# Computing grad_out x gate x w2 of two chunks early and merging two MLP stages, in a transformer block's forward and backward

## The chip, the cores and the metric

The kernel runs on one NeuronCore of a Trainium2 chip. The core has a matrix engine (TensorE, "PE", with its weight loads as "PEld"), a vector engine (VectorE, "DVE"), an activation engine (ScalarE, "ACT"), GpSimd ("POOL"), and SyncE ("SP"), which only issues transfers. Each engine works through its own instructions in order; they meet at semaphores. The metric is the time of one execution on the device, in microseconds (us); lower is better. The kernel before took 2512.56 us in the median of three runs (2511.92 to 2516.4).

## The reference: what is computed

One adaptive-layernorm transformer block, forward and backward, in bf16, with one sequence of S = 2048 tokens, width D = 512, 32 heads of 16, and an MLP of width F = 1792 with squared ReLU:

```
mod = silu(c) @ w_mod               # six rows: sa, ca, ga, sb, cb, gb
h  = layernorm(x) * (1 + ca) + sa
x1 = x + ga * attention(h, wqkv, wo)
h2 = layernorm(x1) * (1 + cb) + sb
r  = relu(h2 @ w1 + b1)
out = x1 + gb * ((r * r) @ w2 + b2)
grads = vjp(block)(grad_out)        # to x, all weights, b1, b2, c, w_mod
```

Of the backward pass this matters here: with s = r * r, the gradient to s is ds = (grad_out * gb) @ w2^T; the one to r's input is dz = 2 * r * ds; the weight gradients are dw2 = s^T @ (grad_out * gb) and dw1 = h2^T @ dz; then dh = dz @ w1^T goes on into the second layernorm. ds needs neither the attention nor the forward MLP: grad_out, the gate gb and w2 are inputs, or follow from inputs at the start. gb has one value for each of the 512 columns.

## The kernel before

Partition size is P = 128. The MLP width is FC = 14 blocks of 128, D is DC = 4 blocks, the tokens are QC = 4 chunks of 512.

**Forward loop** (41.7 to 1006 us). The attention is a list of NF = 512 units (chunk of queries, group of 4 heads, block of 128 keys). In unit u, `fscore` computes the scores of four heads (L560, four matmuls into two PSUM tiles psST, three buffers) and their exponentials on ACT (L562, two ET of 128x1024), and `fpv` multiplies those of unit u-2 with the values (L576). In the same unit other work is slipped in between, in an order that the Python loop fixes by hand (the pools run under a manual schedule, so program order is engine order):
- `plan_tasks` (u = 0 to about 101, only in chunk 0's attention): keys, queries, norms and modulation rows, by `at(u, task)`.
- `later_stage`, when u % 4 == 2: a list of stages. Stage 24 falls on u = 106 (four L705, L706, L707 on DVE: the normalized input of 512 tokens), stage 25 on u = 110 (two reciprocals of one row of 512, L697).
- `turn_weights`, when u % 4 == 0, i = u/4 - 18: transposing DMAs of w1 (i = 2 to 5), of w2 and wo (i = 7 to 10), issued by SP; at i = 12 all three are stored to DRAM.
- `step(u)` moves on the generator `dense_chunk` by one yield, or runs one waiting weight-gradient chain. While chunk c+1's attention runs, `dense_chunk(c)` does chunk c's MLP, forward and backward: 14 steps of pz = w1^T h2 (L398) with relu and square, w2T loaded into the place of w1 (`load_wA`), 14 steps of pds = w2T x gfT (L412; gfT is grad_out * gb, transposed) with dz = 2 * pds * r (L415, which also sums dz for the bias gradient), then dh, the forward product and the attention gradient. A yield of n makes `step` wait n units.
- `steady`, when none of these has issued a product in the unit: two matmuls with zeros that add nothing (L599).

All of this work's products share one PSUM bank (`mm`, one buffer) in the loop. A **chain** (`add_chain`) is one tile of a weight gradient: four accumulating matmuls (L233) of 512, 384 or 256 columns, and its result. Chunk 0 stores the tile to DRAM (`p_st`), chunks 1 and 2 accumulate onto it, and chunk 3 adds it from SBUF (L237 on DVE, after `fetch_part` has loaded it) and writes the output with a DMA issued on ACT's queue. Chains wait in the list `dwq`; `later(n, ...)` issues something n units, or ticks, on.

**Between the loops** (1006 to 1124 us) the last chunk has no attention to hide behind. Here `mm` has four buffers and chains have three banks of their own (pc). `late_finish` and the head of `last_chunk` finish the attention and do the second layernorm. Then stage one: 14 steps of pz (L1336), relu (L1338, ACT), square (L1339, DVE), `tick` (what is due, and one chain) and `turn` (four transposes of s, L1323, evicted on ACT, L1324, and the chain of that block appended). Stage two: 14 steps of pds (L1351), dz (L1354, DVE), bias sum (POOL), `tick`, `turn` of dz. Then dh (L1377), the layernorm gradient, the forward product (L1429) and the attention gradient. `head_loads` issues the first loads of the next loop.

**Backward loop** (1124 to 2380 us): attention's backward by heads, in which ACT (L1601) and DVE (L1617) are both busy; then a final stage. The diff does not touch them.

Of the kernel before, what the change touches and what calls it, by code (L numbers as in the profile page):

```python
# [15 lines left out]
ALU = mybir.AluOpType  # L16
# [18 lines left out]
def kernel(  # L35
# [111 lines left out]
    with ExitStack() as ph:  # L147
# [32 lines left out]
        def later(lag, f, *args):  # L180
            due.append((unit[0] + lag, f, args))
# [108 lines left out]
        def chunk_loads(c):  # L290
            ts = slice(4 * c, 4 * c + 4)
            end = c == QC - 1
            if end:
                L = dict(begun)
            else:
                L = {"w1": load_wA(w1_src, 6), "w1T": load_wB(w1T_st[:], 20)}
                L["g"] = cb.tile([P, 4, D], BF, name="g_c", tag="g_c")
                sp(L["g"][:], g_dram[:, ts, :])
            L["wo"] = ffw.tile([P, DC, D], BF, name="wo_nat", tag="wo")
            sp(L["wo"][:], A_wo.rearrange("(oc p) j -> p oc j", p=P))  # L300
            L["x1"] = cb.tile([P, 4, D], BF, name="x1_c", tag="x1_c")
            sp(L["x1"][:], x_dram[:, ts, :])
            L["gf"] = cb.tile([P, 4, D], BF, name="gf_c", tag="gf")
            L["gfT"] = cb.tile([P, 4, DC, P], BF, name="gfT", tag="gfT")

            def scaled():
                POOL.tensor_tensor(L["gf"][:], L["g"][:], gb_bc.unsqueeze(1).to_broadcast([P, 4, D]), ALU.mult)
                later(6, sp, L["gfT"].rearrange("p t o q -> p (t o) q"), flat(L["gf"]), True)

            def sums():  # L310
                for ti in range(4):
                    rowsum(4, L["g"][:, ti, :], 4 * c + ti)

            if end:
                return L
            later(5, scaled)
            later(16, sums)
            return L

        def dense_chunk(c, O_c, L):  # L320
            ts = slice(4 * c, 4 * c + 4)
            g_c, x1_c, gf_c, gfT, w1_nat, w1T = (L[key] for key in ("g", "x1", "gf", "gfT", "w1", "w1T"))
            a_c = cb.tile([P, 4, D], BF, name="a_c", tag="a_c")
# [71 lines left out]
            for fc in range(FC):  # L395
# [9 lines left out]
                yield 0  # L405
            w2T = load_wA(w2T_st[:], 1)
            yield 3
            dzT = rT
            for fc in range(FC):
                pds = mm()  # L410
                for oc in range(DC):
                    PE.matmul(pds[:], w2T[:, oc, fc * P:(fc + 1) * P], gfT[:, :, oc, :],  # L412
                              start=(oc == 0), stop=(oc == DC - 1))
                db1p = wk.tile([P, 1], F32, name="db1p", tag="db1p")
                DVE.scalar_tensor_tensor(out=dzT[:, fc, :], in0=pds[:], scalar=2.0, in1=rT[:, fc, :],  # L415
                                         op0=ALU.mult, op1=ALU.mult, accum_out=db1p[:])
# [298 lines left out]
        def turn_weights(i):  # L715
            if i == 2:
                turned["1"] = ffw.tile([P, FC, D], BF, name="w1T_0", tag="wB")
                turned["2"] = ffw.tile([P, DC, FF], BF, name="w2T_0", tag="wA")
                turned["o"] = ffw.tile([P, DC, D], BF, name="woT_0", tag="wo")
            if 2 <= i < 6:  # L720
                for fc in range(4 * (i - 2), min(FC, 4 * (i - 2) + 4)):
                    sp(turned["1"][:, fc, :], B_w1[:, fc * P:(fc + 1) * P], True)
            if 7 <= i < 11:
                sp(turned["2"][:, i - 7, :], B_w2[:, (i - 7) * P:(i - 6) * P], True)
                sp(turned["o"][:, i - 7, :], A_wo[:, (i - 7) * P:(i - 6) * P], True)
# [262 lines left out]
        def plan_tasks():  # L988
# [124 lines left out]
            at(67, lambda: mod_cols_of(mm(), 3, 2))  # L1113

        NF = len(funits)

# [34 lines left out]
        with ExitStack() as ph2:  # L1151
# [3 lines left out]
            with tc.manual_schedule(engines={PE.engine, ACT.engine, DVE.engine, SP.engine, POOL.engine}):  # L1155
                fh[0, 0] = (qts[0], kts[0])
                for u in range(NF + 2):
# [75 lines left out]

        def last_chunk(O_c, L, w1T, w2T):
            c = QC - 1
            ts = slice(4 * c, 4 * c + 4)
            g_c, x1_c, gf_c, gfT, w1_nat = (L[key] for key in ("g", "x1", "gf", "gfT", "w1"))
            OT, pas = L["OT"], L["pa"]
# [74 lines left out]
            sT = cb.tile([P, FC, 512], BF, name="sT", tag="sT")  # L1313
            tks = {}

# [17 lines left out]
            for fc in range(FC):  # L1333
                pz = mm()
                for ic in range(DC):
                    PE.matmul(pz[:], w1_nat[:, ic, fc * P:(fc + 1) * P], h2T[:, :, ic, :],  # L1336
                              start=(ic == 0), stop=(ic == DC - 1))
                ACT.activation(rT[:, fc, :], pz[:], AF.Relu, bias=b1col[:, fc:fc + 1])  # L1338
                DVE.tensor_tensor(sT[:, fc, :], rT[:, fc, :], rT[:, fc, :], ALU.mult)  # L1339
                tick()  # L1340
                if fc > 0:
                    turn("s", sT, fc - 1)
            later(3, sp, woT[:], woT_st[:])
            w2_nat = ffw.tile([P, FC, D], BF, name="w2_1", tag="wA")
            for s in range(7):
                later(5 + 2 * s, sp, w2_nat[:, 2 * s:2 * s + 2, :], w2_src[:, 2 * s:2 * s + 2, :])
            dzT = rT
            for fc in range(FC):
                pds = mm()
                for oc in range(DC):  # L1350
                    PE.matmul(pds[:], w2T[:, oc, fc * P:(fc + 1) * P], gfT[:, :, oc, :],  # L1351
                              start=(oc == 0), stop=(oc == DC - 1))
                db1p = wk.tile([P, 1], F32, name="db1p", tag="db1p")
                DVE.scalar_tensor_tensor(out=dzT[:, fc, :], in0=pds[:], scalar=2.0, in1=rT[:, fc, :],  # L1354
                                         op0=ALU.mult, op1=ALU.mult, accum_out=db1p[:])
                POOL.tensor_tensor(db1acc[:, fc:fc + 1], db1acc[:, fc:fc + 1], db1p[:], ALU.add)
                if fc == 7:
                    head_loads()
                tick()
                turn(*(("dz", dzT, fc - 1) if fc else ("s", sT, FC - 1)))  # L1360
            turn("dz", dzT, FC - 1)
            keep["KS"] = kpool.tile([P, TT, QPAD], BF, name="KS_tok", tag="ks")
            POOL.memset(keep["KS"][:, :, D:QPAD], 0.0)
            for i in range(4):
                later(4 + 3 * i, sp, keep["KS"][:, 4 * i:4 * i + 4, 0:D], k_st[:, 4 * i:4 * i + 4, :])
            ACT.activation(tiny[:], onesf[:, 0:1], AF.Exp)
# [127 lines left out]
        with ExitStack() as ph2:  # L1494
            pools["mm"] = ph2.enter_context(tc.tile_pool(name="psM2", bufs=4, space=bass.MemoryType.PSUM))
            with tc.manual_schedule(engines={PE.engine, ACT.engine, DVE.engine, SP.engine, POOL.engine}):
# [11 lines left out]
                O_c = late_finish()  # L1508
                sp(L["gfT"].rearrange("p t o q -> p (t o) q"), flat(L["gf"]), True)
                for i in range(4):  # L1510
# [20 lines left out]

                last_chunk(O_c, L, w1T, w2T)
                for j, row in ((0, 5), (1, 3), (2, 4), (3, 2)):
# [518 lines left out]
```

## Time and profile before

| | us |
|---|---|
| median of three runs | 2512.56 (2511.92 to 2516.4) |
| span of the profiled execution (the page gives no other time of it) | 2513.8 |
| PE busy / ACT busy / DVE busy in the span | 2335.0 / 2302.6 / 1809.7 |
| ET, L562, 1024 times | 942.3 |
| first pz of stage one, first pds of stage two | 1024.38, 1051.90 |
| first dh product, first score of the backward loop | 1077.66, 1124.05 |

How to read it. Times are us from the span's start. A line of groups gives line, engine, operation, tiles with shapes and count, then busy time, mean ns of one, and the idle time just before, with what ended most of it. A line of the timeline gives start and duration; the bracket is the idle time before it and the engine, tile and line that ended it. In a row of stretches each engine has its busy time and, as (x), its instructions; the clock column is the TensorE clock granted, 1.00 being full speed; the DMA share is the mean busy share of 16 queues' engines, with GB/s behind it. Matmuls overlap: four of 128x512 show 1.03 us of busy time, but the next product can start 0.865 us after the first.

### The profile page before, as it was taken

The numbers are of one execution on the slowest core, as the hardware profiler recorded it, in microseconds if no ns is written. First come the engines' busy times: TensorE is split into PE (matmuls) and PEld (weight loads), VectorE is DVE, ScalarE is ACT, GpSimd is POOL, SyncE is SP. The second block draws the span as 40 slices with busy tenths as digits, with TensorE's granted clock in tenths as the row PEclk, the third lists the DMA queues.
The fourth block names the chain that finished last, engine by engine and source line by source line (L and its number), as shares of the span: only waits on it lengthen the run. The fifth ranks groups of instructions, "written<-read, shape, count | busy, mean of one in ns | idle before, by whom it ended". The sixth has DMA issues, their size and how long they took to land.

```text
span 2513.8 us, 49777 instructions
## 1 busy us (share of the span) xinstructions
PE 2335.0 (93%) x18916; PEld 777.9 (31%) x19005; DVE 1809.7 (72%) x2317; ACT 2302.6 (92%) x3577; POOL 348.0 (14%) x370
## 2 busy tenths in 40 slices
PE   7898889989988998999999999999999999999999
PEld 3232223222322323442233322233222323222343
DVE  6555153455435454579999999999998999999872
ACT  7999999999999999539999999999999999999952
POOL 2000000210333142210111101011010110110100
PEclk9999999999999999999999999999999999999999
DMA  6476465356748765969999999999999999999972
GB/s 203 129 193 177 136 131 139 96 160 136 110 88 174 153 131 118 264 211 184 207 203 210 199 198 204 204 201 206 204 200 206 199 195 204 206 199 215 197 254 72
DMA packets 1220981, 447.15 MB, mean 178 GB/s; under 512 B 1096951, under 2 KB 1191607, under 8 KB 1220486
## 3 DMA queue, kind: packets, MB, share of 16 engines
q1 hardware_dynamic: 1192822, 409.11, 81.8%
q0 software_dynamic: 10944, 16.78, 4.5%
q10 hardware_dynamic: 16976, 18.07, 2.8%
q8 instruction: 149, 2.44, 0.4%
q14 instruction: 90, 0.74, 0.1%
HBM read 96.75 MB, written 73.95 MB: 68 GB/s over the span
## 4 chain that ended last, share of the span: by engine, by line
PE 40%; ACT 39%; issue 7%; DVE 7%; DMA 4%; SPq 2%; ACTq 1%; POOL 0%; DVEq 0%; another core or an unknown queue 0%
ACT E_u L1601 24%; ACT ET L562 11%; PE dqacc L1682 5%; PE psST L560 4%; PE psS_A L1595 3%; PE pm L233 3%; PE accVK L1655 2%; ACT dsT L1761 2%; PE oacc L576 2%; PE psS_B L1595 2%; SPq L178 2%; PE psS_C L1595 2%; PE pm L412 2%; PE pdh L1876 2%; PE pwq L1910 2%
## 5 line engine op out<-in xcount | busy, mean ns | idle before, releaser
L1617 DVE TENSOR_TENSOR dS_u<-psD_u,E_u 128x1024 bf16<-128x1024 f32 x1024 | 1186.2, 1219 | 71.2 <-PE psD_u L1615 25.5
L562 ACT ACTIVATE ET<-psST 128x1024 bf16<-128x1024 f32 x1024 | 942.3, 1247 | 25.3 <-PE psST L560 24.7
L1601 ACT ACTIVATE E_u<-psS_A 128x512 bf16<-128x512 f32 x768 | 509.6, 664 | 11.0 <-PE psS_C L1595 8.5
L1601 ACT ACTIVATE E_u<-psS_B 128x512 bf16<-128x512 f32 x768 | 502.6, 654 | 12.5 <-PE psD_u L1615 3.4
L1615 PE MATMUL psD_u<-iv,ido 32*128 32x512 bf16 x2048 | 409.9, 388 | 0.5 <-DVE dS_u L1617 0.2
L560 PE MATMUL psST<-qt_sb,kt_sb 32*128 32x512 bf16 x2048 | 316.5, 387 | 53.0 <-ACT ET L562 46.2
L1601 ACT ACTIVATE E_u<-psS_C 128x512 bf16<-128x512 f32 x512 | 333.7, 652 | 2.7 <-PE psS_B L1595 1.0
L1595 PE MATMUL psS_B<-ik,iq 32*128 32x512 bf16 x768 | 294.9, 384 | 12.5 <-ACT E_u L1601 5.0
L1595 PE MATMUL psS_A<-ik,iq 32*128 32x512 bf16 x768 | 293.4, 382 | 11.1 <-DVE dwlast L237 1.0
L1595 PEld LDWEIGHTS <-iq 32*128 32x128 bf16 x2048 | 130.5, 91 | 316.0 <-issue 299.9
L1655 PE MATMUL accVK<-dS_u,qz 128*32 128x512 bf16 x2048 | 213.0, 390 | 0.5 <-PE psD_u L1615 0.3
L576 PE MATMUL oacc<-ET,vaug 128*32 128x512 bf16 x2048 | 207.8, 396 | 1.9 <-DVE ostage L580 1.9
L1664 PE MATMUL accVK<-E_u,dOs_tok 128*16 128x512 bf16 x2048 | 203.7, 386 | 0.0
L1700 POOL TENSOR_TENSOR dQacc<-dQacc,dqtmp 128x512 f32<-128x512 f32 x64 | 81.3, 1271 | 851.4 <-ACT dqtmp L1695 851.4
L1595 PE MATMUL psS_C<-ik,iq 32*128 32x512 bf16 x512 | 194.6, 380 | 4.2
L560 PEld LDWEIGHTS <-kt_sb 32*128 32x128 bf16 x2048 | 85.4, 91 | 341.0 <-issue 320.4
L1682 PE MATMUL dqacc<-dsT,KS_tok 128*32 128x512 bf16 x2048 | 147.7, 387 | 18.7 <-DMA dsT<-dS_u 4.3
L1761 ACT ACTIVATE dsT<-ptT 128x1024 bf16<-128x1024 bf16 x128 | 145.3, 1135 | 7.0 <-PE ptT L1645 6.4
L251 DVE COPY part<-pm 128x512 f32<-128x512 f32 (+2 forms) x103 | 63.5, 617 | 117.5 <-PE pm L233 106.0
L1615 PEld LDWEIGHTS <-ido 32*128 32x128 bf16 x2048 | 105.0, 91 | 100.7 <-issue 94.5
L1655 PEld LDWEIGHTS <-qz 128*32 128x32 bf16 x2048 | 58.5, 94 | 177.8 <-issue 162.8
L576 PEld LDWEIGHTS <-vaug 128*32 128x32 bf16 x2048 | 53.0, 93 | 121.0 <-issue 121.0
(407 smaller groups left out, 2499.5 us busy)
## 6 DMA issues: line engine op xcount, KB each, us to landing
p_st<-part POOLq DMA_DIRECT2D x36, 256.0 KB, 5.2
kt_sb<-qkT_st SPq DMA_DIRECT2D x124, 64.0 KB
wA<-in_B_w_dram SPq DMA_DIRECT2D x28, 256.0 KB
wB<-w1T_st SPq DMA_DIRECT2D x21, 256.0 KB
wA<-w2T_st SPq DMA_DIRECT2D x21, 256.0 KB
wB<-in_B_w_dram SPq DMA_DIRECT2D x21, 256.0 KB
p_st<-part POOLq DMA_DIRECT2D x25, 192.0 KB, 4.2
p_st<-part SPq DMA_DIRECT2D x18, 256.0 KB
```

The costliest lines, as they stand in the source:

```text
L560: PE.matmul(ps[:, hi, :], kt_sb[r:r + 32, kt * P:(kt + 1) * P], qt_sb[r:r + 32, :], start=True, stop=True, tile_position=(r, 0))
L562: ACT.activation(ET[:, 2 * pair:2 * pair + 2, :], ps[:], AF.Exp, scale=SCALE)
L576: PE.matmul(oacc[32 * hq:32 * hq + 32, :], lhsT, ET[:, hq, :], start=(kt == 0), stop=(kt == TT - 1), tile_position=(0, 32 * hq), skip_grou ...
L1595: PE.matmul(psS[:], st["q"][r:r + 32, qt * P:(qt + 1) * P], st["k"][r:r + 32, kc * 512:kc * 512 + 512], start=True, stop=True, tile_positi ...
L1601: ACT.activation(bst[u][0][:, hq, :], sst.pop((u, hq))[:], AF.Exp, scale=SCALE)
L1615: PE.matmul(psD[:, hi, :], st["do"][r:r + 32, qt * P:(qt + 1) * P], st["v"][r:r + 32, kc * 512:kc * 512 + 512], start=True, stop=True, til ...
L1617: DVE.tensor_tensor(dS_u[:, 2 * pair:2 * pair + 2, :], psD[:], E_u[:, 2 * pair:2 * pair + 2, :], ALU.mult)
L1655: PE.matmul(cur["vk"][32 * hq:32 * hq + 32, :], hst[hg]["qz"][:, qt, hq, :], bst[u][1][:, hq, :], start=(qt == 0), stop=False, tile_positi ...
L1664: PE.matmul(acc[32 * hq:32 * hq + DH, :], dOs_tok[:, qt, (hg * 4 + hq) * DH:(hg * 4 + hq + 1) * DH], E_u[:, hq, :], start=False, stop=(qt ...
L1682: PE.matmul(acc[32 * hq:32 * hq + 32, :], KS_tok[:, kc * 4 + kt, h * DH:h * DH + 32], tT[:, :, hq * 4 + kt, :], start=(kt == 0), stop=(kt ...
L1700: POOL.tensor_tensor(dst2, dst, tmp[:], ALU.add)
L1761: ACT.activation(dst, pt[:], AF.Identity)
```

## The change

ds of chunks 2 and 3 is computed during chunk 0's attention, in the units u = 102 to 129, and kept in DRAM (`ds_st`). For that:
- the gate's columns (`gate_cols`, u = 78), the transposed grad_out of chunks 2 and 3 (`turned_grads`, u = 91, four transposing DMAs on SP) and its scaling (`scale_grads`, u = 97 to 100, four DVE operations) are new in the plan;
- `early_ds` in each of 28 units: four matmuls of 128x512 into the `mm` bank, a copy to bf16 on DVE, and a store of every third block (ten DMAs on SP), chunk 3 first, then chunk 2;
- `turn_weights` turns w2 first (u = 80, 84), then wo (88, 92), then w1 (100 to 112).

For chunk 2, `dense_chunk` loads ds in place of w2T and has no pds products; it yields at every second step only. For chunk 3, between the loops, ds takes the place of w2T, and the two stages of 14 steps are one: pz, relu, square, dz from SBUF, bias sum, tick, turn s, tick, turn dz. The loads of w2 and KS, of parts and `head_loads` are shifted to fit. Chunks 2 and 3 have no gfT. In chunk 3's attention, once the dense work has ended, a ripe chain runs only if more than nine wait, and in the last two units only if more than six do.

In the built program the following order comes out. On DVE: the copies of u = 102 to 105, then L705 to L707, the copies of 106 to 109, then both L697, then the other copies. After the last score two chains run instead of three. Six chains (two of 384, four of 256) are left behind the loop instead of eleven (seven and four); six run during the layernorm in both. In the merged stage 12 chains of 512 and 12 of 384 columns run; in steps 1 to 3 the chain of s stands directly behind its own turn; from step 4 on each step is pz, chain, turn of s, chain, turn of dz. ACT's order in such a step is relu, the output DMA of the chain before, the eviction (tk) of s, the output DMA of this step's first chain, tk of dz.

```diff
+    ds_st = dram.tile([2, P, FC, 512], BF, name="ds_st")
...
+            turned_early = c == QC - 2
...
-            w2T = load_wA(w2T_st[:], 1)
+            if turned_early:
+                ds = ffw.tile([P, FC, 512], BF, name="ds_c", tag="wA")
+                for s in range(7):
+                    later(1 + s, sp, ds[:, 2 * s:2 * s + 2, :], ds_st[0][:, 2 * s:2 * s + 2, :])
+            else:
+                w2T = load_wA(w2T_st[:], 1)
...
-                yield 0
+                if not turned_early or fc % 2 == 1:
+                    yield 0
...
+            def gate_cols():
+                pc = mm()
+                for q in range(4):
+                    for ic in range(DC):
+                        PE.matmul(pc[:, q:q + 1], wmod_slice(5)[:, ic, q * P:(q + 1) * P], siluc_col[:, ic:ic + 1],
+                                  start=(ic == 0), stop=(ic == DC - 1))
+                gbf = wk.tile([P, DC], BF, name="gbf", tag="gbf", bufs=1)
+                DVE.tensor_copy(gbf[:], pc[:, 0:4])
+                DVE.tensor_copy(modcol[:, 5, :], gbf[:])
+
+            def turned_grads():
+                T["gT"] = cb.tile([P, FC, 512], BF, name="gT", tag="sT")
+                for oc in range(DC):
+                    sp(T["gT"][:, 2 * oc:2 * oc + 2, :].rearrange("p a q -> p (a q)"),
+                       grad_out[0][512 * (QC - 2):, oc * P:(oc + 1) * P], True)
+
+            def scale_grads(oc):
+                part = T["gT"][:, 2 * oc:2 * oc + 2, :]
+                DVE.tensor_scalar(part, part, modcol[:, 5, oc:oc + 1], None, ALU.mult)
+
+            def early_ds(c, fc):
+                if fc % 3 == 0:
+                    T["ds"] = cb.tile([P, 3, 4, P], BF, name="dsE", tag="tk", bufs=5)
+                pds = mm()
+                for oc in range(DC):
+                    PE.matmul(pds[:], turned["2"][:, oc, fc * P:(fc + 1) * P], T["gT"][:, 2 * oc + c, :],
+                              start=(oc == 0), stop=(oc == DC - 1))
+                tk = T["ds"].rearrange("p f t q -> p f (t q)")
+                DVE.tensor_copy(tk[:, fc % 3, :], pds[:])
+                if fc % 3 == 2 or fc == FC - 1:
+                    f0 = fc // 3 * 3
+                    later(1, sp, ds_st[c][:, f0:fc + 1, :], tk[:, 0:fc + 1 - f0, :])
+
+            at(78, gate_cols)
+            at(91, turned_grads)
+            for oc in range(DC):
+                at(97 + oc, scale_grads, oc)
+            for k in range(2 * FC):
+                at(102 + k, early_ds, 1 - k // FC, k % FC)
...
-                if ripe:
+                if ripe and (fqueue or dense or len(dwq) > 9):
...
-                    elif dwq and u >= NF - 2:
+                    elif dwq and u >= NF - 2 and len(dwq) > 6:
...
-                later(7 + i, fetch_part, FC + i)
+                later(2 + i, fetch_part, FC + i)
...
                 DVE.tensor_tensor(sT[:, fc, :], rT[:, fc, :], rT[:, fc, :], ALU.mult)
+                db1p = wk.tile([P, 1], F32, name="db1p", tag="db1p")
+                DVE.scalar_tensor_tensor(out=dzT[:, fc, :], in0=ds[:, fc, :], scalar=2.0, in1=rT[:, fc, :],
+                                         op0=ALU.mult, op1=ALU.mult, accum_out=db1p[:])
+                POOL.tensor_tensor(db1acc[:, fc:fc + 1], db1acc[:, fc:fc + 1], db1p[:], ALU.add)
+                if fc == 10:
+                    head_loads()
                 tick()
                 if fc > 0:
                     turn("s", sT, fc - 1)
-            later(3, sp, woT[:], woT_st[:])
+                tick()
+                if fc > 0:
+                    turn("dz", dzT, fc - 1)
+            sp(woT[:], woT_st[:])
             w2_nat = ffw.tile([P, FC, D], BF, name="w2_1", tag="wA")
             for s in range(7):
-                later(5 + 2 * s, sp, w2_nat[:, 2 * s:2 * s + 2, :], w2_src[:, 2 * s:2 * s + 2, :])
-            dzT = rT
-            for fc in range(FC):
-                pds = mm()
-                for oc in range(DC):
-                    PE.matmul(pds[:], w2T[:, oc, fc * P:(fc + 1) * P], gfT[:, :, oc, :],
-                              start=(oc == 0), stop=(oc == DC - 1))
...
-                if fc == 7:
-                    head_loads()
-                tick()
-                turn(*(("dz", dzT, fc - 1) if fc else ("s", sT, FC - 1)))
+                later(1 + s, sp, w2_nat[:, 2 * s:2 * s + 2, :], w2_src[:, 2 * s:2 * s + 2, :])
+            tick()
+            turn("s", sT, FC - 1)
             turn("dz", dzT, FC - 1)
...
-                w2T = kpool.tile([P, DC, FF], BF, name="w2T_1", tag="ks")
-                for s in range(4):
-                    sp(w2T[:, s, :], w2T_st[:, s, :])
+                ds = kpool.tile([P, FC, 512], BF, name="ds_1", tag="ks")
+                for s in range(7):
+                    sp(ds[:, 2 * s:2 * s + 2, :], ds_st[1][:, 2 * s:2 * s + 2, :])
```

More of the change, by code (lines that the diff above doesn't have):

```diff
@@ L303, in chunk_loads @@
             L["gf"] = cb.tile([P, 4, D], BF, name="gf_c", tag="gf")
-            L["gfT"] = cb.tile([P, 4, DC, P], BF, name="gfT", tag="gfT")
+            if c < QC - 2:
+                L["gfT"] = cb.tile([P, 4, DC, P], BF, name="gfT", tag="gfT")
             def scaled():
                 POOL.tensor_tensor(L["gf"][:], L["g"][:], gb_bc.unsqueeze(1).to_broadcast([P, 4, D]), ALU.mult)
-                later(6, sp, L["gfT"].rearrange("p t o q -> p (t o) q"), flat(L["gf"]), True)
+                if c < QC - 2:
+                    later(6, sp, L["gfT"].rearrange("p t o q -> p (t o) q"), flat(L["gf"]), True)
             def sums():
@@ L321, in dense_chunk @@
             ts = slice(4 * c, 4 * c + 4)
-            g_c, x1_c, gf_c, gfT, w1_nat, w1T = (L[key] for key in ("g", "x1", "gf", "gfT", "w1", "w1T"))
+            g_c, x1_c, gf_c, w1_nat, w1T = (L[key] for key in ("g", "x1", "gf", "w1", "w1T"))
+            turned_early = c == QC - 2
             a_c = cb.tile([P, 4, D], BF, name="a_c", tag="a_c")
@@ L409, in dense_chunk @@
             for fc in range(FC):
-                pds = mm()
-                for oc in range(DC):
-                    PE.matmul(pds[:], w2T[:, oc, fc * P:(fc + 1) * P], gfT[:, :, oc, :],
-                              start=(oc == 0), stop=(oc == DC - 1))
+                if turned_early:
+                    dsrc = ds[:, fc, :]
+                else:
+                    pds = mm()
+                    for oc in range(DC):
+                        PE.matmul(pds[:], w2T[:, oc, fc * P:(fc + 1) * P], L["gfT"][:, :, oc, :],
+                                  start=(oc == 0), stop=(oc == DC - 1))
+                    dsrc = pds[:]
                 db1p = wk.tile([P, 1], F32, name="db1p", tag="db1p")
-                DVE.scalar_tensor_tensor(out=dzT[:, fc, :], in0=pds[:], scalar=2.0, in1=rT[:, fc, :],
+                DVE.scalar_tensor_tensor(out=dzT[:, fc, :], in0=dsrc, scalar=2.0, in1=rT[:, fc, :],
                                          op0=ALU.mult, op1=ALU.mult, accum_out=db1p[:])
                 POOL.tensor_tensor(db1acc[:, fc:fc + 1], db1acc[:, fc:fc + 1], db1p[:], ALU.add)
-                yield 0
+                if not turned_early or fc % 2 == 1:
+                    yield 0
                 if fc % 3 == 2 or fc == FC - 1:
@@ L719, in turn_weights @@
                 turned["o"] = ffw.tile([P, DC, D], BF, name="woT_0", tag="wo")
-            if 2 <= i < 6:
-                for fc in range(4 * (i - 2), min(FC, 4 * (i - 2) + 4)):
+            if 2 <= i < 4:
+                for oc in (2 * i - 4, 2 * i - 3):
+                    sp(turned["2"][:, oc, :], B_w2[:, oc * P:(oc + 1) * P], True)
+            if 4 <= i < 6:
+                for oc in (2 * i - 8, 2 * i - 7):
+                    sp(turned["o"][:, oc, :], A_wo[:, oc * P:(oc + 1) * P], True)
+            if 7 <= i < 11:
+                for fc in range(4 * (i - 7), min(FC, 4 * (i - 7) + 4)):
                     sp(turned["1"][:, fc, :], B_w1[:, fc * P:(fc + 1) * P], True)
-            if 7 <= i < 11:
-                sp(turned["2"][:, i - 7, :], B_w2[:, (i - 7) * P:(i - 6) * P], True)
-                sp(turned["o"][:, i - 7, :], A_wo[:, (i - 7) * P:(i - 6) * P], True)
             if i == 12:
@@ L1113, in plan_tasks @@
             at(67, lambda: mod_cols_of(mm(), 3, 2))
+            def gate_cols():
[18 more added lines that the diff above has]
+                    T["ds"] = cb.tile([P, 3, 4, P], BF, name="dsE", tag="tk", bufs=5)
+                pds = mm()
+                for oc in range(DC):
+                    PE.matmul(pds[:], turned["2"][:, oc, fc * P:(fc + 1) * P], T["gT"][:, 2 * oc + c, :],
+                              start=(oc == 0), stop=(oc == DC - 1))
+                tk = T["ds"].rearrange("p f t q -> p f (t q)")
[5 more added lines that the diff above has]
+            at(91, turned_grads)
+            for oc in range(DC):
+                at(97 + oc, scale_grads, oc)
+            for k in range(2 * FC):
+                at(102 + k, early_ds, 1 - k // FC, k % FC)
         NF = len(funits)
@@ L1232, in copy_const, with last_chunk @@
             ACT.activation(dst, onesf[:, 0:1].to_broadcast([P, n]), AF.Identity, scale=value)
-        def last_chunk(O_c, L, w1T, w2T):
+        def last_chunk(O_c, L, w1T, ds):
             c = QC - 1
             ts = slice(4 * c, 4 * c + 4)
-            g_c, x1_c, gf_c, gfT, w1_nat = (L[key] for key in ("g", "x1", "gf", "gfT", "w1"))
+            g_c, x1_c, gf_c, w1_nat = (L[key] for key in ("g", "x1", "gf", "w1"))
             OT, pas = L["OT"], L["pa"]
@@ L1313, in last_chunk @@
             sT = cb.tile([P, FC, 512], BF, name="sT", tag="sT")
+            dzT = rT
             tks = {}
@@ L1342, in last_chunk @@
                     turn("s", sT, fc - 1)
-            later(3, sp, woT[:], woT_st[:])
+                tick()
+                if fc > 0:
+                    turn("dz", dzT, fc - 1)
+            sp(woT[:], woT_st[:])
             w2_nat = ffw.tile([P, FC, D], BF, name="w2_1", tag="wA")
             for s in range(7):
-                later(5 + 2 * s, sp, w2_nat[:, 2 * s:2 * s + 2, :], w2_src[:, 2 * s:2 * s + 2, :])
-            dzT = rT
-            for fc in range(FC):
[L1349 to L1356, printed above, removed]
-                if fc == 7:
-                    head_loads()
-                tick()
-                turn(*(("dz", dzT, fc - 1) if fc else ("s", sT, FC - 1)))
+                later(1 + s, sp, w2_nat[:, 2 * s:2 * s + 2, :], w2_src[:, 2 * s:2 * s + 2, :])
+            tick()
+            turn("s", sT, FC - 1)
             turn("dz", dzT, FC - 1)
@@ L1364, in last_chunk @@
             for i in range(4):
-                later(4 + 3 * i, sp, keep["KS"][:, 4 * i:4 * i + 4, 0:D], k_st[:, 4 * i:4 * i + 4, :])
+                later(9 + i, sp, keep["KS"][:, 4 * i:4 * i + 4, 0:D], k_st[:, 4 * i:4 * i + 4, :])
             ACT.activation(tiny[:], onesf[:, 0:1], AF.Exp)
@@ L1508 @@
                 O_c = late_finish()
-                sp(L["gfT"].rearrange("p t o q -> p (t o) q"), flat(L["gf"]), True)
                 for i in range(4):
@@ L1530, in head_loads @@
                     later(16, spread_qz, 0)
-                last_chunk(O_c, L, w1T, w2T)
+                last_chunk(O_c, L, w1T, ds)
                 for j, row in ((0, 5), (1, 3), (2, 4), (3, 2)):
```

## The prediction

> **What bounds the kernel now.** I read the shares of the span first, then the costliest groups, then the stretches that the change touches. On the page one group carries the forward loop (busy, mean ns of one, idle before it and its releaser):
>
> ```profile
> L562 ACT ACTIVATE ET<-psST 128x1024 bf16<-128x1024 f32 x1024 | 942.3, 1247 | 25.3 <-PE psST L560 24.7
> ```
>
> The exponentials (ET, two a unit) are busy 942.3 of the loop's some 964 us (41.7 to 1006): in the loop ACT sets the end. A unit of the loop takes about 1.84 us (24 ET in 22.1 us from 242). The stretches show where there is room, and what a pause costs (columns: stretch, its length, busy PE, PEld, DVE, ACT, POOL, granted clock, DMA share, GB/s):
>
> ```profile
> 199.40:202.80 3.40, 2.29 (x14) 0.64 (x13) 2.39 (x5) 0.93 (x2) 0.00 (x0) 0.52 0.10 19
> 202.80:206.20 3.40, 3.40 (x22) 1.01 (x18) 1.01 (x2) 2.75 (x3) 0.00 (x0) 0.50 0.48 105
> ...
> 260.00:280.00 20.00, 16.97 (x110) 4.20 (x110) 0.00 (x0) 20.00 (x23) 0.62 (x1) 0.91 0.60 233
> ...
> 1024.00:1052.00 28.00, 27.23 (x163) 14.38 (x165) 12.23 (x26) 18.54 (x33) 4.26 (x5) 0.94 1.07 268
> 1052.00:1078.00 26.00, 25.89 (x173) 14.41 (x173) 18.24 (x44) 10.51 (x16) 2.82 (x15) 1.00 0.89 272
> ```
>
> At 260 to 280 us, where the new products go, DVE is idle and ACT full. From 1024 to 1078 us, the two MLP stages that become one, PE is full and the others are not: work taken from PE there shortens the kernel. The first two rows are a pause in the loop, which these lines of the timeline (start, length, engine, instruction, idle before it and its releaser) explain:
>
> ```profile
> 196.25 1.36 DVE L705 TENSOR_SCALAR tmpT<-tmpT,mean,rstd 128x512 bf16<-128x512 bf16 x4
> ...
> 200.51 0.58 PE L1069 MATMUL ptk<-identb,sP 128*128 128x128 bf16 x4 [2.28 <-DVE tokP L1077]
> ...
> 202.69 1.94 ACT L562 ACTIVATE ET<-psST 128x1024 bf16<-128x1024 f32 x2 [2.48 <-PE psST L560]
> 205.28 1.94 ACT L562 ACTIVATE ET<-psST 128x1024 bf16<-128x1024 f32 x2 [0.65 <-PE psST L560]
> ...
> 236.07 1.38 DVE L705 TENSOR_SCALAR tmpT<-tmpT,mean,rstd 128x512 bf16<-128x512 bf16 x4
> ...
> 239.89 6.54 DVE L697 RECIPROCAL racc<-modbc 1x512 f32<-1x512 bf16 x2
> ```
>
> A block of six DVE operations (L705 to L707, 3.8 us) stood before the PSUM copy that PE waited for: PE stopped for 2.28 us, ACT lost 2.48 + 0.65, and the clock was 0.52 and 0.50 in the two stretches. The same block comes again at 236.07, and then 6.54 us of reciprocals; there PE waits for no DVE work, so they cost nothing today.
>
> **The change in the loop (u = 102 to 129, some 238 to 290 us).** 28 units get four matmuls 128x512 and a DVE copy out of the single mm bank, in place of the filler pair. Matmuls (4 x 0.216 = 0.87 us) and a copy (0.69, by the copy of the same size at L348) and the hand-overs fit a unit: the chunks' units with the same pattern (L412, 862.84, 864.72, 866.61) start 1.88 us apart, those with a chain 1.80. So 0 to 28 x 0.04 = 1.1 us; I take 0. What does not fit is the order on DVE. In the built program it reads: copies of u=102 to 105, L705 to L707, copies of u=106 to 109, both reciprocals, the rest. Engines run in order, and PE's next ds product waits for the bank, with the next score queued behind it and ACT behind that.
> - Stall one: the copy of u=106 starts 3.85 us after that of u=105 ends, where it would have 1.84 - 0.69 = 1.15: 2.7 late. The row above gives ACT a cushion of about 0.5 us: -2.2 remain. By the other blocks of L705 (213.46 and 221.58, PE idle 1.32 and 1.33) ACT lost 0.7 and 1.5, and 3.1 in the row above: ends 0.7 and 3.1.
> - Stall two: 6.54 - 1.15 = 5.4 late, less 0.5: **4.9 us**.
> - The clock after them: at full clock a ds unit holds PE for 0.45 (scores) + 0.39 (L576) + 0.87 = 1.71 us, at half clock 3.4, so a 3.4 us stretch at half clock does one unit instead of 1.85: 1.6 us lost. One such stretch behind each stall: 3.2 us (ends: none, and two each, 6.4, as the two rows above show).
> - `gate_cols` (16 one-column matmuls, two small DVE copies, u=78): 0.3 us, ends 0 and 0.5. The four gT transposes, the reordered weight transposes and ten stores are on SP, which issues each in 1.3 to 2.0 us; gT is issued near 226 us and used from 230, so 0. Scaling gT (4 DVE operations) precedes the first ds product: 0.
> - Chunk 2 drops 14 x 4 matmuls and ends 7 units earlier. ACT is full there (L562), so PE's saving is worth 0; the dz operation reads SBUF, 0.75 by L1408 for 0.69.
>
> Loop: 2.2 + 4.9 + 3.2 + 0.3 = **+10.6 us** (5.6 to 15.3). ACT has no spare time later, so nothing of it is caught up.
>
> On the clock, the row says: pause of 2.28 us, then 0.52 and 0.50. [...]
>
> **The change between the loops.** Of PE's work from the first pz (1024.38) to the first dh product (1077.66) these go: 56 matmuls of L1351, 14 x 0.865 = 12.1 us, and some chains: now 14 of 512, 10 of 384 and 4 of 256 columns run there (0.865, 0.65, 0.44 us each: 20.3), after it 12 of 512 and 12 of 384 (18.2). The pz (12.1) and 28 turns (0.22 each, 6.2) stay. Together **-14.3 us**: 50.8 of issue become 36.5 (the stretch lasts 53.3; what it waits at its start, I leave as it is). What comes late next:
>
> ```profile
> 1041.26 0.69 ACT L1338 ACTIVATE rT<-pm,b1col 128x512 bf16<-128x512 f32 x1 [0.27 <-PE pm L1336]
> ...
> 1041.98 0.43 DVE L1339 TENSOR_TENSOR sT<-rT 128x512 bf16<-128x512 bf16 x1 [0.70 <-ACT rT L1338]
> ...
> 1045.34 0.60 ACT L1324 ACTIVATE tk<-ptk 128x512 bf16<-128x512 bf16 x1 [1.34 <-PE pm L1336]
> ...
> 1045.84 0.68 ACT L1338 ACTIVATE rT<-pm,b1col 128x512 bf16<-128x512 f32 x1
> ...
> 1062.78 0.69 DVE L1354 SCALAR_TENSOR_TENSOR rT<-pm,rT 128x512 bf16<-128x512 f32 x1 [0.46 <-PE pm L1351]
> ...
> 1063.40 0.55 DVE L237 TENSOR_TENSOR dwbuf<-pc,dwbuf 128x384 bf16<-128x384 f32 x1
> ...
> 1063.98 0.35 ACTq L188 DMA_DIRECT2D out_dram<-dwbuf  x1
> ```
>
> - Steps 1 to 3: the chain of s(fc-1) stands right behind its own transposes, so PE waits for their way through ACT (transpose 0.39, tk 0.60, hand-overs): 1.2 us each, **+3.6** (ends 0 and 3.6).
> - Steps 4 to 13 have a ring through ACT, whose order is relu, store of the chain before, tk of s, store of this step's first chain, tk of dz. By the starts above: relu to sT 0.72, sT to dz 0.38, dz to the chain's addition 0.62, to its store 0.58, store to tk 0.38, tk to the next relu 0.50: **3.2 us a step**. PE's own steps (pz, two transposes, two chains) are five of 2.6, three of 3.03, two of 2.82: 27.8 for ten. The ring makes 32: **+4.2** (ends 0, if a store never waits, and 7.4, with the full durations 0.69 + 0.43 + 0.83 + 0.62 + 0.35 + 0.60 = 3.52).
> - ds_1 takes the place of w2T_1 on SP at equal bytes, on queues that show a share of 0.89 to 1.07: 0. The constant fill (L1232 on ACT, 1.9 us) lies in the stage either way: 0 to 1.9, I take 0.
> - One chain less after the last score (1005 to 1008 us): 0.87 and part of its copy, -1.2. Fewer chains behind the stage: -0.2.
>
> Sum: -14.3 + 3.6 + 4.2 - 1.4 = **-7.9 us** (-15.7 to -2.8).
>
> **Net** +10.6 - 7.9 = +2.7. The page has the span alone (2513.8 us), no time of its own beside it; it stands 1.2 above the median of the runs, 2512.56, and inside their spread (2511.92 to 2516.4). I add the sum to the median: **2515.3 us**, no change within 0.2% (5.0 us, about what a measurement of this kernel can tell from none).
>
> **Rivals.**
> - *Faster (chance 0.18):* the merged stage is PE's alone: no ring and no waits, -15.7, and the clock holds after the stalls, so the loop costs 10.6 - 3.2 = 7.4. For it: four pm banks and three pc banks let PE run ahead. Against: ACT's order. 2512.56 - 8.3 = 2504.3.
> - *Slower (0.34):* half clock in the loop. Each stall leaves two stretches of 3.4 us at half clock, as at 199.4 to 206.2, and not one: 3.2 us more, 2518.5. It decides from 2.3 us more than forecast, that is from three and a half such stretches. For it: ds units ask more of PE than the units of that row. Against: clock 0.64 in a single stretch after the block at 221.58.
> - *The loop costs its least,* 5.6, with the stage as forecast: -2.3, 2510.3, inside no change.
> - *The merge does not do what it says:* the stage keeps its 53 us since part fetches or stores bind. For it: their bytes are nearly as before in less time, and the DMA share is already near 1. Against: no L237 addition in either stage waits for a fetch. The loop's loss then stands with -1.4 alone: 2521.8, counted in the slower 0.34.
>
> **Numbers.** No change 0.48, faster 0.18, slower 0.34. The range: from the faster rival (2505) to the stage that gains nothing (2522).
>
> **What would show it.** Right: ACT idle before ET near u=107 (2 to 4 us) and u=111 (5 to 7), each with PE released by a DVE copy and a clock near 0.5; first pz to first dh product 44 to 46 us; relu to relu 3.2 us in steps 4 to 13 with PE idle released by ACT. Wrong: no ET gap near the reciprocals; or steps of 2.6 to 3.0 us with PE full (faster); or over 50 us in the stage (slower).

## The result and the profile after

The changed kernel is **slower**: 2528.35 us in the median of ten runs (2515.22 to 2533.97), beside 2514.36 us (2511.92 to 2524.71) for the kernel before in ten. The ratio is 1.0042, with a 95% interval of 1.0025 to 1.0060: 6 to 15 us, 10.6 us in the middle. The prediction said no change (2515.3 us, range 2505 to 2522). Its share for slower was 0.34, and the median lies above the range.

The spans of two single profiled executions are a poor measure here (2513.8 and 2522.5 us). From the first exponential of the backward loop (E_u) to the end, where no kernel of this study differs, the thirteen profiled executions took 1381 to 1401 us. So below a trace is read up to that E_u, and verdicts on the whole come from the timed runs. Where two points of the forward loop are compared, they are the copies of ostage on DVE (L580 before, L594 after): one ends each group of 16 units, 32 in each kernel, so that the same units stand against each other. The stretch from u=127 to u=431, in which the kernels differ little, took 567.5 to 577.9 us over the thirteen, so its +1.4 below is within what traces differ by.

| stretch, us | before | after | difference | predicted |
|---|---|---|---|---|
| ostage of u=95 to ostage of u=127 (early ds) | 58.2 | 68.3 | +10.1 | +10.6 with the gate columns |
| u=127 to u=431 | 570.6 | 572.0 | +1.4 | 0 |
| u=431 to u=511 (chunk 2's second half) | 147.4 | 157.1 | **+9.7** | **0** |
| last PV product to first pz | 17.9 | 17.0 | -0.9 | -1.2 |
| first pz to first dh product | 53.3 | 48.5 | -4.8 | -6.5 |
| first dh product to first E_u | 46.8 | 49.8 | +3.0 | -0.2 |

The line of the exponentials on the page of the changed kernel (busy, mean, idle before and its releaser):

```profile
L576 ACT ACTIVATE ET<-psST 128x1024 bf16<-128x1024 f32 x1024 | 943.4, 1246 | 43.2 <-PE psST L574 42.6
```

Their work is the same, 943.4 us; their idle time has grown from 25.3 to 43.2, all of it waiting for scores. Where the first ten of these lie is shown by the timeline of the changed kernel (the copy at 248.29 is the one that L719 to L721, here in L705's place, delayed; L711 are the reciprocals):

```profile
243.87 0.69 DVE L1160 CAST dsE<-pm 128x512 bf16<-128x512 f32 x1 [1.14 <-PE pm L1157]
244.47 1.38 DVE L719 TENSOR_SCALAR tmpT<-tmpT,mean,rstd 128x512 bf16<-128x512 bf16 x4
...
248.29 0.68 DVE L1160 CAST dsE<-pm 128x512 bf16<-128x512 f32 x1
...
249.02 1.02 PE L1157 MATMUL pm<-gT,w2T 128*128 128x512 bf16 x4 [2.50 <-DVE dsE L1160]
...
250.69 1.94 ACT L576 ACTIVATE ET<-psST 128x1024 bf16<-128x1024 f32 x2 [2.18 <-PE psST L574]
253.61 5.61 ACT L576 ACTIVATE ET<-psST 128x1024 bf16<-128x1024 f32 x6 [0.98 <-PE psST L574]
...
255.46 6.54 DVE L711 RECIPROCAL racc<-modbc 1x512 f32<-1x512 bf16 x2
...
262.60 1.86 PE L1157 MATMUL pm<-gT,w2T 128*128 128x512 bf16 x4 [5.32 <-DVE dsE L1160]
...
265.12 1.94 ACT L576 ACTIVATE ET<-psST 128x1024 bf16<-128x1024 f32 x2 [5.91 <-PE psST L574]
267.70 62.44 ACT L576 ACTIVATE ET<-psST 128x1024 bf16<-128x1024 f32 x68 [0.64 <-PE psST L574]
```

Read it as a relay: DVE's block ends, the copy that waited behind it runs, PE's ds product (idle 2.50 and 5.32 us for that copy) gets the bank, then the score behind it, then ACT. ACT's four pauses are 2.18 + 0.98 + 5.91 + 0.64 = 9.7 us. After 267.70 it runs 68 ET without a pause: the other ds units cost nothing.

### The profile page after: what moved, and what is told of

Read it like the earlier page. It is cut to its first block, busy times and chain, and to the rows that moved or that the text cites. A ratio compares the mean times of both kernels' runs of the same rounds, so it can differ in the third digit from the quotient of the medians.

```text
span 2522.5 us, 49846 instructions
## 1 busy us (share of the span) xinstructions
PE 2338.0 (93%) x18979; PEld 775.6 (31%) x18979; DVE 1832.4 (73%) x2356; ACT 2298.6 (91%) x3572; POOL 349.1 (14%) x370
## 4 chain that ended last, share of the span: by engine, by line
PE 39%; ACT 38%; DVE 8%; issue 8%; DMA 5%; ACTq 1%; SPq 0%; POOL 0%; DVEq 0%; POOLq 0%
ACT E_u L1655 23%; ACT ET L576 10%; PE dqacc L1736 4%; PE psST L574 4%; PE psS_A L1649 3%; PE pm L234 2%; PE accVK L1709 2%; PE oacc L590 2%; ACT dsT L1815 2%; PE psS_B L1649 2%; PE psS_C L1649 2%; PE pdh L1930 2%; PE pwq L1964 2%; PE pm L402 2%; PE pm L501 2%
## 5 line engine op out<-in xcount | busy, mean ns | idle before, releaser
L576 ACT ACTIVATE ET<-psST 128x1024 bf16<-128x1024 f32 x1024 | 943.4, 1246 | 43.2 <-PE psST L574 42.6
L590 PEld LDWEIGHTS <-vaug 128*32 128x32 bf16 x2048 | 53.3, 93 | 126.0 <-issue 126.0
```

What stands on the lines that cost most here:

```text
L576: ACT.activation(ET[:, 2 * pair:2 * pair + 2, :], ps[:], AF.Exp, scale=SCALE)
L590: PE.matmul(oacc[32 * hq:32 * hq + 32, :], lhsT, ET[:, hq, :], start=(kt == 0), stop=(kt == TT - 1), tile_position=(0, 32 * hq), skip_grou ...
```

## The experiments

**Theory after the result.** (a) In the loop the early products cost about 10 us, only where a DVE block stands before their copies. (b) Chunk 2's shortened backward half costs several us in chunk 3's attention. (c) Between the loops the gain is small because PE waits where it worked before. Rivals: the 28 units cost by their number; the loss at u=431 to 511 is one run's accident; the merged stage is limited elsewhere.

Eleven kernels were timed in three groups, on three chips, each group beside the kernel before on the same chip (median 2518.0 to 2518.5 us over its 29 to 35 runs there). Ratios are to the kernel before.

### loop_only: the early products alone

The kernel before, plus `ds_st`, the new functions with their `at(...)` lines, and the new order in `turn_weights`; what is stored is not used.

> The kernel before, with the early products alone added: gate columns, turned and scaled grad_out, 28 units of ds with copy and store, weight transposes in the changed kernel's order; what it stores is not used. Theory (the copies queue on DVE behind L705 to L707 and the two reciprocals, ACT starves): 9 to 11 us slower than before, ET idle of about 2, 1 and 6 us at u=107 to 113 and little elsewhere. Rival (the 28 units cost by their number, through the one PSUM bank): also slower, but the idle time is spread over u=102 to 129. Rival (the loop hides it): within 2 us.

Measured: 1.0030 (1.0012 to 1.0048), so 7.5 us (3 to 12; 9 to 11 expected). From u=95 to 127 it took 68.2 us for 58.2. In the timeline of loop_only the pauses of ACT in this stretch are

```profile
251.34 1.94 ACT L563 ACTIVATE ET<-psST 128x1024 bf16<-128x1024 f32 x2 [2.65 <-PE psST L561]
253.81 5.61 ACT L563 ACTIVATE ET<-psST 128x1024 bf16<-128x1024 f32 x6 [0.53 <-PE psST L561]
265.51 1.94 ACT L563 ACTIVATE ET<-psST 128x1024 bf16<-128x1024 f32 x2 [6.09 <-PE psST L561]
```

the same three places, with 9.3 us together, and u=431 to 511 took 147.6 us, as before. So the early products do not cause the loss at the loop's end.

### ds_skip and skip_recip: products kept out of the blocked units

```diff
-            for k in range(2 * FC):
-                at(102 + k, early_ds, 1 - k // FC, k % FC)
+            ds_units = [u for u in range(102, 135) if u not in (106, 107, 110, 111, 112)]
+            for k in range(2 * FC):
+                at(ds_units[k], early_ds, 1 - k // FC, k % FC)
```

In skip_recip the list is 102 to 132 without 110, 111 and 112 only.

> The changed kernel, with no ds product in the units 106, 107, 110, 111 and 112, where DVE does L705 to L707 and the reciprocals; five units more behind 129 make up for it. Theory: 8 to 10 us faster than the changed kernel (ET idle near u=107 to 113 under 2 us). Rival (28 units through one bank): within 2 us of the changed kernel.

> The changed kernel with no ds product in the units 110, 111 and 112 alone, so that only the reciprocals are stepped round and the block of L705 to L707 still stands before a copy. Theory (each block costs what it delays the copy, and the clock behind it): of the some 10 us that the five skipped units brought, 6 to 7 here; ET idle of about 3 us stays near u=107. Rival (one half-clock stretch behind either block is most of it): 3 us or less, or all 10.

ds_skip measured 1.0003 (0.9983 to 1.0022), 10 us better than the changed kernel's 1.0042 (8 to 10 expected); skip_recip 1.0025 (1.0007 to 1.0043). From u=95 to 127 they took 58.2 and 61.8 us. The timelines, ds_skip first, then skip_recip:

```profile
235.01 35.96 ACT L576 ACTIVATE ET<-psST 128x1024 bf16<-128x1024 f32 x39
```

```profile
251.83 1.94 ACT L576 ACTIVATE ET<-psST 128x1024 bf16<-128x1024 f32 x2 [2.52 <-PE psST L574]
254.44 15.89 ACT L576 ACTIVATE ET<-psST 128x1024 bf16<-128x1024 f32 x17 [0.67 <-PE psST L574]
```

With all five units skipped ACT runs 39 ET on end, through both blocks, with the same 28 products in nearly the same place: the rival of 28 units that cost by their number falls. The reciprocals were worth 68.3 - 61.8 = 6.5 us of the stretch (6 to 7 expected), the block of L705 to L707 61.8 - 58.2 = 3.6. The timed difference of skip_recip to the changed kernel is smaller, 4 us, with intervals that overlap; the two were timed on different chips.

### yield_each and skip_yield: chunk 2 keeps its place

```diff
-                if not turned_early or fc % 2 == 1:
-                    yield 0
+                yield 0
```

yield_each is the changed kernel with this, skip_yield has the five skipped units too. In both more chains are left behind the loop, and part of w1's gradient comes out wrong: by the program's order the leftover chains write over fetched parts in the ring of six. They serve here for what their traces show, not as versions to use.

> The changed kernel, with chunk 2 yielding at each of the 14 dz steps as before, so that its later work keeps its place against the attention's loads. Theory (the seven units saved put the loads of w2 behind those of the next head group, and PE waits for them): 4 to 7 us faster than the changed kernel, no wait of PE for the w2 load in chunk 3's attention, ET idle between u=432 and 488 back to about 1 us. Rival (that idle time is one run's accident): same as the changed kernel within 2 us.

> Both edits, the skipped units and the yield at each step. Theory: the losses in the loop go, the gain between the loops stays (3 to 6 us by the two traces): 2 to 6 us faster than the kernel before. Rival (the gain is eaten by the new wait of the backward loop's first E_u, 2.7 us): same as before within 1 us.

Measured: 1.0049 (1.0030 to 1.0067) and 1.0002 (0.9987 to 1.0017). The loop did what theory (b) said: u=431 to 511 took 148.3 and 147.6 us, and PE had no wait for the w2 load. But the total did not improve, a miss: the first pz to the first dh product grew to 56.4 and 57.6 us (48.5 in the changed kernel). The seven units that chunk 2 saves had run chains; with them gone, five more chains came into the merged stage (17 of 384 and 256 columns for 12). So the units saved do carry chains, and the loss at the loop's end comes from when chunk 2's later work stands, not from less of it. A version was needed that keeps both.

### skip_wait7: the place kept, the units given to chains

```diff
             if c == QC - 2:
+                yield 7
                 begun["w1"] = load_wA(w1_src, 1)
```

With the five skipped units; the yield stands behind the dz steps, which go by two as in the changed kernel.

> The changed kernel with the skipped units, and with chunk 2 waiting seven units behind its 14 dz steps (in which only chains run), so that its later work stands against the attention's loads as in the kernel before while no more chains are left behind the loop. Theory (the second loss of the loop is chunk 2's later work met out of step by the loads and by DVE): ET idle from u=432 to the loop's end about 1 to 2 us instead of 5 to 9, the stretch between the loops as in the changed kernel, 4 to 6 us faster than with the skipped units alone, so 3 to 6 us faster than before. Rival (that idle time is accident or comes from the yields by two): same as with the skipped units alone within 2 us.

Measured: 0.9974 (0.9952 to 0.9995), so faster than before, and 7 us better than ds_skip's ratio, with intervals that overlap a little. u=431 to 511: 148.9 us, for 153.7 in ds_skip. Over all kernels the two groups do not overlap: those in which chunk 2's later work comes seven units early (after, ds_skip, skip_recip, skip_sp) took 157.1, 153.7, 153.8 and 151.5 us there, the nine others 147.3 to 149.6. The accident is ruled out; the loss is 5.8 us in the mean (154.0 less 148.2).

One thing that goes out of step is seen on SP and PE. The changed kernel, then the kernel before:

```profile
936.85 2.05 SPq L141 DMA_DIRECT2D kt_sb<-qkT_st  x4
938.96 3.31 SPq L141 DMA_DIRECT2D qt_sb<-qkT_st  x4
...
942.96 4.21 SPq L179 DMA_DIRECT2D wB<-in_B_w_dram  x7
...
956.01 0.59 PE L501 MATMUL pm<-wB,sT 128*128 128x512 bf16 x2 [2.39 <-DMA wB<-in_B_w_dram]
957.24 1.94 ACT L576 ACTIVATE ET<-psST 128x1024 bf16<-128x1024 f32 x2 [2.18 <-PE psST L574]
```

```profile
934.91 3.74 SPq L178 DMA_DIRECT2D wB<-in_B_w_dram  x7
...
948.95 0.82 PE L487 MATMUL pm<-wB,sT 128*128 128x512 bf16 x3
```

Before, w2's load is issued 14.0 us ahead of its first product. After, it stands on SP behind the loads of the next head group (kt_sb, qt_sb), and its first product (949.35) comes 6.4 us after the issue; a later piece of it is late by 2.39 us, and ACT loses 2.18 there. This is one place, and not the steady one: the w2 wait was 2.4, 0.9 and 0.2 us in after, ds_skip and skip_sp, and skip_recip has none. What all four have is a wait for a part copy, some 14 us ahead of the last ostage copy. In the changed kernel:

```profile
1011.92 0.56 DVE L252 COPY part<-pm 128x384 f32<-128x384 f32 x1 [2.81 <-DMA p_st<-part]
1012.53 0.30 PE L628 MATMUL pm<-identf,rrows 28*128 28x28 f32 x2 [2.49 <-DVE part L252]
1013.28 1.94 ACT L576 ACTIVATE ET<-psST 128x1024 bf16<-128x1024 f32 x2 [2.02 <-PE psST L574]
```

Chains stand in successive units there, and DVE's copy waits for the store of an earlier part (p_st). PE's wait is 2.5, 2.1, 2.4 and 1.2 us in the four and at most 0.7 in the nine others; ACT's pauses in the last 20 us before the ostage copy of u=511 add up to 2.4 to 3.7 us in the four and to 0.3 to 1.1 in the others. So some 2 of the 5.8 us lie here, and no run takes this wait away by itself. How the rest divides among the w2 load, waits of PE for DVE and the clock (last section) differs from profile to profile and stays open. PE's 1.83 us for ostage behind DVE's layernorm block at 933 is no part of it: it is 1.65 in the kernels that wait seven units. It is absent where chunk 2 yields at every dz step (yield_each, skip_yield, and before), so it goes with the yields by two.

### The merged stage: skip_wait7_sp, skip_wait7_lag2, skip_wait7_both, skip_sp, before_sp

```diff
-                    later(1, sp if late else ACT.dma_start, dst, res)
+                    later(1, sp, dst, res)
```

is the edit "sp" (the output stores go to SP's queue). "lag2" makes the chain of s ripe a tick later:

```diff
-                    dwq.append(add_chain(c, 1, fc, D, lambda ti: tk[:, f, ti, :], ...
+                    dwq.append(add_chain(c, 2, fc, D, lambda ti: tk[:, f, ti, :], ...
```

> skip_wait7 with the merged stage's output stores issued on SP's queue instead of ACT's. Theory (from step 7 on the stage is a ring through ACT, 3.4 us a step, because a store waits there for DVE's addition with the next eviction behind it): steps of 2.6 to 3.1 us with PE full, 2.5 to 4 us off the merged stage. Rival (the ring only moves: SP waits with the part fetches behind it): the same length or longer, with waits of DVE for parts.

> skip_wait7 with each chain of s in the merged stage ripe one tick later, so that it does not stand right behind its own transposes. Theory (PE waits 5 to 6 us in steps 1 to 3 for the chain's operand): those waits go, the merged stage is 4 to 6 us shorter, with 0.9 us given back by the chain that is left behind it. Rival (ACT is the bound from the start): under 2 us.

> skip_wait7 with both edits of the merged stage. Theory: 38 to 40 us from the first pz to the first dh product instead of 48.5, that is PE's own 36.5 and little more; 8 to 12 us faster than the kernel before. Rival (DVE is the next bound, 2.4 us of work a step and in order): 42 us or more in that stretch, 4 to 6 us faster than before.

> The kernel before, with the last chunk's output stores issued on SP's queue instead of ACT's, as a control. Theory (the stores hurt only where ACT's ring is longer than PE's step, which the two stages of before do not have: PE is full there): within 3 us of the kernel before. Rival (stores on ACT's queue cost wherever they stand): as much faster as the same edit made the merged kernel, 5 us or more.

> The changed kernel with the five skipped units and the stores on SP's queue, without the seven units of waiting in chunk 2. Theory (the two edits act in different places and add): 3 to 7 us faster than before, some 4 us slower than with the waiting as well. Rival (the waiting brought nothing): as fast as with it.

| kernel | ratio (95%) | first pz to first dh | first dh to first E_u |
|---|---|---|---|
| before | 1 | 53.3 | 46.8 |
| after | 1.0042 (1.0025 to 1.0060) | 48.5 | 49.8 |
| skip_wait7 | 0.9974 (0.9952 to 0.9995) | 48.9 | 50.2 |
| skip_wait7_sp | **0.9948 (0.9931 to 0.9966)** | 43.7 | 50.0 |
| skip_wait7_lag2 | 0.9996 (0.9974 to 1.0017) | 46.1 | 52.5 |
| skip_wait7_both | 0.9954 (0.9935 to 0.9974) | 38.3 | 53.3 |
| skip_sp | 0.9981 (0.9965 to 0.9997) | 42.1 | 50.6 |
| before_sp | 1.0004 (0.9989 to 1.0018) | 53.1 | 46.9 |

The longest waits in the merged stage of the changed kernel (waiting line, releaser, total us, times, longest), PE's and then ACT's:

```profile
PE pc L234 <- ACT tk L1382: 6.3, 4, 2.9
```

```profile
ACT tk L1382 <- DVE dwbuf L238: 8.5, 5, 1.9
```

and one turn of the ring in its last steps:

```profile
1079.17 0.68 ACT L1396 ACTIVATE rT<-pm,b1col 128x512 bf16<-128x512 f32 x1
1079.74 0.60 ACT L1382 ACTIVATE tk<-ptk 128x512 bf16<-128x512 bf16 x1
1081.75 0.36 ACTq L189 DMA_DIRECT2D out_dram<-dwbuf  x1
1082.21 0.60 ACT L1382 ACTIVATE tk<-ptk 128x512 bf16<-128x512 bf16 x1 [1.87 <-DVE dwbuf L238]
1082.70 0.68 ACT L1396 ACTIVATE rT<-pm,b1col 128x512 bf16<-128x512 f32 x1
```

ACT stands idle for 1.87 us between the two evictions, because the store at 1081.75 waits for DVE's addition; relu to relu is 3.53 us. pz starts at 1076.02, 1079.37, 1082.86 and 1086.20: 3.3 to 3.5 us a step. With the stores on SP the same stretch of skip_wait7_sp shows no such wait on ACT, and pz starts at 1054.12, 1057.16, 1059.77 and 1062.38, 2.6 to 3.0 us a step, PE's own time. The stage is 5.3 us shorter (2.5 to 4 expected), the kernel 6.5 us faster by the ratios (0.9974 to 0.9948, with intervals that overlap). The same edit without the waiting goes the same way: skip_sp's ratio is 5.5 us below ds_skip's. In before_sp, whose stages have PE full, it is worth nothing that can be told from zero, as the theory said: the stores cost where ACT's ring is the longest.

lag2 met its expectation in the stage only with sp: 38.3 us in skip_wait7_both, close to PE's 36.5 (35.6 without the chain of 0.87 that lag2 leaves behind the stage). But that is paid back behind it: first dh product to first E_u takes 53.3, and the ratio is no better than with sp alone. Without sp, lag2 is a miss: it shortens the stage by 2.8 us (4 to 6 expected), lengthens what follows by 2.3, and the timed ratio is no better but 5.5 us worse (intervals overlap). The expected 8 to 12 us came (11.6), though the edit of lag2 adds nothing to them.

skip_sp is 4.8 us faster than before (3 to 7 expected). Against skip_wait7_sp (0.9981 and 0.9948) it repeats what the seven units of waiting are worth: some 8 us by the ratios, with intervals that touch, and 3.8 by the traces from u=431 to 511 (151.5 and 147.7). The best version, skip_wait7_sp, is faster than both kernels: 2509.18 us in the median, 13 us (9 to 17) below the kernel before.

## Why the prediction was wrong, point by point

- **"Stall one", "stall two" and the clock behind them, +10.3: right.** The stretch grew by 10.1 us; the reciprocals took 6.5 of it (4.9 + 1.6 predicted), the block of L705 to L707 3.6 (2.2 + 1.6). PE's pauses were 2.50 and 5.32 for 2.7 and 5.4. Without a stretch at half clock behind stall one the forecast's terms make 2.2 of the 3.6, with one 3.8. The clock was at 0.50 for one stretch behind stall one (250.0 to 253.4) and for two behind stall two (260.2 to 267.0), but PE itself still waited until 262.60, so that the price of one stretch was about right. The sentence that ACT catches nothing up later held too as far as the traces tell: the next stretch, to u=431, gave nothing back. The upper end of the loop's cost, 15.3, comes to 14.9 from the ends that are named; nothing rests on it.
- **"Chunk 2 drops 14 x 4 matmuls and ends 7 units earlier. ACT is full there (L562), so PE's saving is worth 0": this step failed.** It weighed what is removed, and not that everything behind it moves: 5.8 us were lost in the mean (4.1 to 9.7 above the kernel before), shown by the wait of seven units that takes them away. No row of before's waits could show it; what could have was that w2's load is placed by a lag of units on a queue that the attention's loads share at u % 16 == 4, and that chains in successive units share a few part buffers, each busy until its store has landed (DVE's copy at 1011.92 waited 2.81 us for one). The prediction gave this term no bounds at all.
- **"-14.3 us: 50.8 of issue become 36.5": right as a sum of PE's work.** skip_wait7_both, with most of the waits taken away and one chain of 0.87 less in the stage, needs 38.3. That it is a gain in time was the step's weak point, which the waits below measure.
- **Steps 1 to 3, +3.6: too small.** PE waited 0.69, 1.65 and 2.91 us there, 5.3 in all; the last of these has ACT waiting for DVE work as well (dpad's memset), which was left out.
- **The ring through ACT, 3.2 us a step, +4.2: the mechanism right, the place not.** It appears from step 9 on, at 3.3 to 3.5 us, and once at step 7 (4.0); steps 4 to 6 and 8 ran at PE's 2.6 to 3.0. Taking its cause away is worth 5.3 us of the stage.
- **The stretch behind the stage, -0.2: wrong by 3.** The first E_u of the changed kernel waits for a store that the kernel before had finished:

```profile
1138.29 0.37 PE L1649 MATMUL psS_A<-ik,iq 32*128 32x512 bf16 x1 [0.95 <-DVE dwlast L238]
...
1141.41 0.60 ACT L1655 ACTIVATE E_u<-psS_A 128x512 bf16<-128x512 f32 x1 [9.87 <-DMA d_st<-dltT]
```

  Its score starts at 1138.29, and E_u 3.12 us later; in the kernel before it is 0.41 us, so 2.7 us are lost. SP's transposes of dOs_c waited there 6.5 us for the store of dx (3.3 before). The loads of w2 and KS, which were moved into that stretch, are not enough to explain it: skip_wait7_sp has them too, and there SP waits 2.9 us (5.6 in skip_wait7), and E_u starts 0.42 us after its score. The same holds over all kernels: E_u starts 2.2 to 5.4 us after its score in the seven merged ones with stores on ACT's queue, and 0.4 in the three with the stores on SP. How these stores delay the one of dx is not shown, and the whole stretch is still 50.0 us with them on SP: what holds it then stays open.
- **The rivals.** The slower one named half clock in the loop, two stretches behind each stall; there was one behind the first, and the early products cost what the forecast said, so that was not the cause. "The loop's loss with a stage that gains nothing" came nearest in size (2521.8), but the stage gained 4.8 us. The faster rival's price (a stage that is PE's alone) was nearly had in skip_wait7_both, with stores and chains moved, but what follows the stage grew by 3.3 us beside skip_wait7_sp.

Taken together, from single traces: +10.1 (early ds) + 5.8 (chunk 2's place) - 2.7 (from the last PV product to E_u) = 13.2, beside a timed 10.6 (6 to 15). The prediction's +2.7 lacks the second term and has the third at -7.9: the gain between the loops was over-counted by 5.2 us, 1.7 of it in the stage and 3.2 behind it, where the wait of E_u had no term.

## What to carry to other kernels

Work put into an idle engine of this loop cost by the longest thing that the engine already did between two of its turns, so look for blocks there (two small reciprocals, 6.54 us of DVE, were worth 6.5 us of the stretch) and step round them. Shortening one stage under a fixed schedule moves all that follows against loads and blocks that do not move (5.8 us here): keep its place and give the time to other work, as seven units of chains did here. When two stages that fill one engine are merged, write down the in-order ring of every other engine, and keep stores that wait for results off the queue that the evictions need (5.3 us of the merged stage here).

## What the runs showed of the hardware that was not expected

The granted clock fell without any long pause of PE. Stretches of the changed kernel in chunk 3's attention (stretch, length, busy PE, PEld, DVE, ACT, POOL, clock, DMA share, GB/s):

```profile
868.00:871.40 3.40, 2.40 (x18) 0.77 (x18) 2.54 (x7) 3.40 (x5) 2.07 (x5) 0.97 1.11 272
871.40:874.80 3.40, 3.25 (x12) 0.64 (x9) 1.43 (x6) 3.25 (x4) 1.72 (x4) 0.50 1.24 175
874.80:878.20 3.40, 3.40 (x17) 0.77 (x17) 1.02 (x2) 1.94 (x2) 0.84 (x1) 0.52 0.78 144
```

PE was busy for 2.40 us of the 3.40 before the fall, and its longest pause there was 0.53 us (869.59 to 870.12); the units there do dz steps without a product, and in the one that ends its group `steady` adds no filler either. The clock was then near half for two stretches, and ACT lost 0.92 and 0.87 us. Behind the early products' first pause, of 2.50 us, it was 0.59 (249.4 to 252.8); behind the pause of 2.28 us in the row of before it was 0.52 (199.4 to 202.8). The length of a pause does not decide by itself. In the kernel before PE stood idle for 2.61 us, up to 804.61, and the clock stayed at full speed, 1.00, round it:

```profile
800.30:807.10 6.80, 4.12 (x32) 1.28 (x29) 6.49 (x10) 4.45 (x6) 4.74 (x5) 1.00 0.57 137
804.61 0.59 PE L347 MATMUL pm<-wo_nat,OT 128*128 128x512 bf16 x2 [2.61 <-DVE a_c L348]
```

So of these three pauses of 2.28 to 2.61 us two were followed by a clock near half and one was not; what decides it was not tested here. Stall one was followed by 0.59, 0.53 and 0.64 (249.4 to 252.8 us) in the changed kernel, loop_only and skip_recip, the traces of it in which the clock was read.
